# A 48-row first transform on quarters of the array, and expert weights loaded in pieces into buffers that the last batch frees

## The chip, the cores and the metric

The kernel runs on one core of a Trainium2 chip. The metric is device time in microseconds (us) of one execution. The core has TensorE (PE), VectorE (DVE), ScalarE (ACT), GpSimd (POOL) and SyncE (SP, here a queue that issues DMAs); 16 DMA engines carry data for all queues.

## What is computed

Three layers follow one another (shortened; the inputs are float32):

```python
X = np.fft.rfft(x, axis=1)                     # x: 8 x 3072 x 256
Yr = X.real @ w_r - X.imag @ w_i + b_r
Yi = X.real @ w_i + X.imag @ w_r + b_i
...                                            # both shrunk towards 0 by 0.01
y = np.fft.irfft(Y, n=3072, axis=1)            # 24576 tokens of 256
logits = y @ phi                               # 32 slots, 4 for each of 8 experts
slot_input = softmax(logits, 0).T @ y
slot_out[e] = np.maximum(slot_input[e] @ w1[e], 0) @ w2[e]   # 256 -> 1024 -> 256
z = softmax(logits, 1) @ slot_out
out = (silu(z @ w_gate) * (z @ w_val)) @ w_out # 256 -> 1536 -> 256
```

## The kernel before

**First half, up to about 584 us of the profile.** Eight batches of 3072 x 256 pass through a pipeline, one after another and overlapping. For each batch the 3072 points of a column are seen as 96 x 32. *Stage a* (`stage_a`, L586) is a float32 matmul with a fixed table `fwd`: 96 rows deep, 128 columns wide, 512 moving columns; it gives the 96-point transform of sixteen of the 256 columns, in one bank of the ring "ac" (two banks, shared with stage c). A DVE transpose (`turn`, L591) moves each bank into the buffer `chan`. A batch has 16 such pairs, p = 0 to 15. *Stage c* (L612) takes `chan` as weights and multiplies with the table `cm`, which finishes the transform; ACT and DVE split the result into a high and a low part (tiles `xg`, `sf`, `sg`). *Stage b* (L700, "pb") multiplies by the mixing weights in groups of three matmuls of 128 x 512 in a faster float format. Then follow the shrinking (ACT, and a join on POOL or DVE, L771), the product with `phi` (L797, four strips of 32 columns of the array side by side), DMAs that lay `yt` out as `yi` (L826), and per batch the logits, softmax and sums for the slots (L865 to L1122, L1103 in strips again). Float32 matmuls leave two records each in the trace, those of stage b one.

x is loaded by SP (L571), four tiles of 96 rows x 64 columns per batch, ring "xq" of two. The tables `cm` and `fwd` and the buffer `chan` lie in `apool`; x tiles in `xpool`.

**Expert weights.** w1 and w2 are 8 MB each. `load_w1` (L427) fetches a whole expert of w1 (1 MB) on POOL's queue: three into the room of `xpool`, freed after the last stage a, five into that of `apool`, freed after the last batch's stage c. `load_w2` (L432) fetches an expert of w2, also on POOL, into tiles that the last batch has left. POOL issues some of the last batch's yi copies too, in the same queue. Every queue tracks its DMAs with eight semaphores in turn, so that a DMA waits for the eighth before it.

**After the slots** (`after_slots`, to about 612 us) the experts run: L1435 with w1, a transpose (L1448), L1460 with w2. **Second half** (from 612 us): 576 steps of the gated layer, bound by PE, with their own loads. It keeps its text in the change.

**What sets the order.** The work of the first half is a list of tasks with the data they need; the table `ORDER` gives the sequence in which they are recorded, for all engines together, and each engine runs its own in that sequence. A negative entry picks the second engine of a task that has two. Waits follow from the data. `HOLD` tasks are dummy matmuls (L1387) that fill gaps near the end of the first half.

Of the kernel before, what the change touches and what calls it, by code (L numbers as in the profile page):

```python
# [23 lines left out]
R2 = 32  # L24
NCH = 24
# [7 lines left out]
def dft_tables():  # L33
# [7 lines left out]
    n1 = np.arange(R1)  # L41
    n2 = np.arange(R2)
    k2 = np.arange(R2)
    sign = np.where(k2 >= R2 // 2, -1.0, 1.0)
    alt1 = np.where(n1 % 2 == 0, 1.0, -1.0)
    alt2 = np.where(n2 % 2 == 0, 1.0, -1.0)
    k1 = np.array([[j, 23 + j] for j in range(NCH)])
    k1[0] = (0, 47)

    fwd = np.zeros((R1, 4, 32))  # L50
    mix = np.zeros((4, R2, NCH, 2, 2, R2))
    for j in range(NCH):
        for h in range(2):
            if j == 0 and h == 0:
                fwd[:, 0, 0] = 1.0
                fwd[:, 1, 0] = alt1
                for i in range(R2):
                    if i == 0:
                        mix[0, :, j, 0, h, 0] = 1.0
                        continue  # L60
                    src = 0 if i < 16 else 1
                    k = 96 * i if i < 16 else 48 + 96 * (i - 16)
                    a = 2 * np.pi * ((n2 * k) % n) / n
                    mix[src, :, j, 0, h, i] = np.cos(a)
                    mix[src, :, j, 1, h, i] = -np.sin(a)
                continue
            a = 2 * np.pi * ((n1 * k1[j, h]) % R1) / R1
            fwd[:, 2 * h, j] = np.cos(a)
            fwd[:, 2 * h + 1, j] = -np.sin(a)
            a = 2 * np.pi * ((n2[:, None] * (k1[j, h] + 96 * k2)[None, :]) % n) / n  # L70
            mix[2 * h, :, j, 0, h, :] = np.cos(a)
            mix[2 * h + 1, :, j, 0, h, :] = np.sin(a)
            mix[2 * h, :, j, 1, h, :] = -np.sin(a) * sign
            mix[2 * h + 1, :, j, 1, h, :] = np.cos(a) * sign
# [85 lines left out]
for _n, _w in (  # L160
# [11 lines left out]
FWD = 136  # L172
# [190 lines left out]
def kernel(  # L363
# [83 lines left out]
    def phase1():  # L447
# [1248 lines left out]
```

## Time and profile before

| what | us |
|---|---|
| runs | 1691.08, 1693.27, 1694.23; median 1693.27 |
| profiled execution | 1693.74 |
| its span in the trace | 1691.6 |
| PE busy in the span | 1662.7 (98%) |
| DVE, ACT, POOL busy | 1296.0, 980.7, 312.5 |
| start of the first matmul | 8.13 |
| start of the gated layer's first matmul | 612.05 |

The profile shows one execution. The rows below come from several of its views: the page (totals), windows (busy time of each engine in a stretch), the timeline (instructions in order, equal neighbours merged with a count), groups by line, and DMA issues. A matmul's own busy time overlaps the next one's, so the time that one costs is read from the starts of those around it. A name in brackets behind a row is what the instruction waited for.

### The profile page before, as it was taken

The page shows a single profiled execution, that of the slowest core. Times are in us where ns is not written, and L with a number is a line of the kernel's source. Part 1 is how long each engine was busy: PE and PEld are TensorE (multiplying, and loading weights), DVE is VectorE, ACT ScalarE, POOL GpSimd, SP SyncE. Part 2 cuts the span into 40 slices and gives each one's busy share as a digit, 9 for nine tenths or more (in the row PEclk, how much of TensorE's full clock was granted, in tenths as well). Part 3 has the DMA queues.
Part 4 walks back from the last instruction along what each step waited for, and adds up shares of the span by engine and source line. Part 5 has one row for each costly group of instructions (what it writes and reads, how often), then busy time and mean ns, then how long its engine had stood idle before and what let it go on. Part 6 is the DMA issues. An engine that isn't in the chain of part 4 may idle for free.

```text
span 1691.6 us, 23302 instructions
## 1 busy us (share of the span) xinstructions
PE 1662.7 (98%) x8178; PEld 1284.8 (76%) x8178; DVE 1296.0 (77%) x2203; ACT 980.7 (58%) x1830; POOL 312.5 (18%) x360
## 2 busy tenths in 40 slices
PE   7999999999999889999999999999999999999998
PEld 4677776776777558888888888888888888888886
DVE  5788888888778458778777777777777777877776
ACT  2655664655657246666656655665666656655664
POOL 1234433334444521100200200200010110110000
PEclk9999999999999999999999999999999999999999
DMA  9465666766556981311311311311230131131111
GB/s 193 88 139 120 123 123 144 138 142 122 126 132 216 310 200 26 81 26 26 81 19 20 82 25 26 70 37 25 41 66 15 24 81 26 25 72 26 25 26 25
DMA packets 260036, 139.94 MB, mean 83 GB/s; under 512 B 210224, under 2 KB 243728, under 8 KB 259920
## 3 DMA queue, kind: packets, MB, share of 16 engines
q1 hardware_dynamic: 246592, 105.03, 31.0%
q0 software_dynamic: 12272, 33.17, 7.2%
q8 instruction: 65, 1.06, 0.3%
q10 hardware_dynamic: 1056, 0.26, 0.1%
q14 instruction: 51, 0.42, 0.1%
HBM read 72.74 MB, written 40.50 MB: 67 GB/s over the span
## 4 chain that ended last, share of the span: by engine, by line
PE 94%; DMA 3%; DVE 1%; POOL 1%; ACT 0%; issue 0%; SPq 0%; DVEq 0%; ACTq 0%
PE o L1572 47%; PE pb L700 11%; PE pg L1547 8%; PE pv L1548 8%; PE ac L586 7%; PE ac L612 5%; PE ch L797 1%; PE ch L865 1%; PE ch L1055 1%; DMA w1s<-in_moe_w_dram 1%; PE ch L1103 1%; DMA w2s<-in_moe_w_dram 1%; PE ch L925 1%; PE ch L1011 1%; PE po L1460 1%; DMA xq<-in_x_dram 0%
## 5 line engine op out<-in xcount | busy, mean ns | idle before, releaser
L1572 PE MATMUL o<-hh,wo 128*128 128x512 f32 x2304 | 722.5, 395 | 0.0
L1550 ACT ACTIVATE sg<-pg 128x512 f32<-128x512 f32 x576 | 344.6, 598 | 413.8 <-PE pg L1547 413.8
L1552 DVE TENSOR_TENSOR h<-sg,pv 128x512 f32<-128x512 f32 x576 | 393.2, 683 | 248.6 <-ACT sg L1550 245.3
L1572 PEld LDWEIGHTS o<-hh,wo 128*128 128x128 f32 x2304 | 434.2, 188 | 100.8
L1572 PE MATMUL o<-hl,wo 128*128 128x512 f32 x1152 | 453.8, 394 | 0.0
L1560 DVE TENSOR_TENSOR hl<-h,hh 128x512 fp32r<-128x512 f32 x576 | 396.7, 689 | 0.1
L1559 ACT ACTIVATE hh<-h 128x512 fp32r<-128x512 f32 x576 | 359.4, 624 | 0.3 <-DVE h L1552 0.2
L1572 PEld LDWEIGHTS o<-hl,wo 128*128 128x128 f32 x1152 | 216.1, 188 | 51.9
L1547 PE MATMUL pg<-cst,gstk 96*128 96x512 f32 x576 | 227.7, 395 | 0.0
L1548 PE MATMUL pv<-cst,gstk 96*128 96x512 f32 x576 | 226.1, 393 | 0.6 <-DVE gstk L1533 0.6
L700 PE MATMUL pb<-xg,whl 128*128 128x512 f32 x576 | 179.3, 441 | 0.0
L700 PEld LDWEIGHTS pb<-xg,whl 128*128 128x128 f32 x576 | 105.3, 189 | 46.5 <-issue 25.1
L1548 PEld LDWEIGHTS pv<-cst,gstk 96*128 96x128 f32 x576 | 109.7, 190 | 25.9 <-DVE gstk L1533 0.9
L1547 PEld LDWEIGHTS pg<-cst,gstk 96*128 96x128 f32 x576 | 108.1, 188 | 25.7 <-DVE gstk L1533 0.8
L771 POOL TENSOR_TENSOR yt<-r,yt 128x512 f32<-128x512 f32 x74 | 96.6, 1305 | 153.5 <-ACT yt L762 103.2
L591 DVE STREAM_TRANSPOSE chan<-ac 128x512 f32<-128x512 f32 x128 | 89.8, 708 | 34.1 <-PE ac L586 29.8
L1608 POOL TENSOR_TENSOR e<-e,rs 96x256 f32<-96x256 f32 x28 | 22.6, 834 | 498.8 <-DVE rs L1605 498.8
L586 PE MATMUL ac<-xq,fwd 96*128 96x512 f32 x224 | 110.3, 598 | 1.2 <-DVE chan L591 0.7
L612 PEld LDWEIGHTS ac<-cm,chan 128*128 128x128 f32 x768 | 101.0, 196 | 12.1 <-issue 4.5
L612 PE MATMUL ac<-cm,chan 128*128 128x128 f32 x768 | 105.3, 283 | 0.0
L700 PE MATMUL pb<-sg,whl 128*128 128x512 f32 x288 | 86.7, 425 | 0.0
L634 ACT ACTIVATE sf<-ac 128x256 f32<-128x256 f32 x96 | 36.5, 381 | 78.5 <-PE ac L612 74.4
(151 smaller groups left out, 1481.1 us busy)
## 6 DMA issues: line engine op xcount, KB each, us to landing
out_dram<-ob SPq DMA_DIRECT2D x190, 128.0 KB, 2.8
yi<-yt SPq DMA_DIRECT2D x368, 64.0 KB, 2.1
xq<-in_x_dram SPq DMA_DIRECT2D x28, 768.0 KB, 8.1
cst<-c_scr POOLq DMA_DIRECT2D x72, 128.0 KB, 3.1
w1s<-in_moe_w_dram POOLq DMA_DIRECT2D x8, 1024.0 KB, 9.0
w2s<-in_moe_w_dram POOLq DMA_DIRECT2D x8, 1024.0 KB, 10.9
x<-in_x_dram SPq DMA_DIRECT2D x4, 768.0 KB, 10.1
cv<-in_moe_w_gate_dram SPq DMA_DIRECT2D x6, 512.0 KB, 6.0
```

What stands on the lines that cost most here:

```text
L586: nc.tensor.matmul(out=pt, lhsT=fwd[:, 8 - 8 * dh:136 - 8 * dh], rhs=T[kq][:, :, d1:d1 + 16], start=True, stop=True)
L591: nc.vector.transpose(out=chan[:, 12 * dh:12 * dh + 16, d0:d0 + 16, :].rearrange("p j d i -> p d j i"), in_=T[ka].rearrange("p n d -> p d n"),
L612: nc.tensor.matmul(out=pt[:, :, q:q + 2, i // 2, :], lhsT=chan[:, 16 * dh + j // 2, :, j % 2], rhs=cm[:, j, :].rearrange("p (c h k) -> p c ...
L700: nc.tensor.matmul(out=pt, lhsT=w[:, dh, m, es], rhs=xx, start=m != 1 and dh == 0 and n == 0, stop=dh == 1 and n == 2, skip_group_check=True,)
L771: e.tensor_sub(out=part(), in0=quarters(T[kr]), in1=part())
L1547: nc.tensor.matmul(out=pg, lhsT=gstk[:, 0, f * 128:(f + 1) * 128], rhs=rhs, start=True, stop=True)
L1548: nc.tensor.matmul(out=pv, lhsT=gstk[:, 1, f * 128:(f + 1) * 128], rhs=rhs, start=True, stop=True)
L1550: nc.scalar.activation(out=sg, in_=pg, func=AF.Silu)
L1552: nc.vector.tensor_mul(out=h, in0=sg, in1=pv)
L1559: nc.scalar.activation(out=hh, in_=h, func=AF.Copy)
L1560: nc.vector.tensor_sub(out=hl, in0=h, in1=hh.bitcast(F32))
L1572: nc.tensor.matmul(out=po_t[0][k], lhsT=w[:, f % 4, k * 128:(k + 1) * 128], rhs=a, start=(f == 0 and m == 0), stop=(f == NF - 1 and m == 2 ...
```

## The change

The 3072 points are now seen as 48 x 64. A first transform has 48 rows and 64 columns, so that it fits a quarter of the array; a batch's x comes in tiles of two row blocks (rows 0 to 47 and 64 to 111 of the tile), with two halves of 384 KB loaded apart, ring "xq" of three. For batches 1 to 7 one task issues four quarter matmuls, which fill two banks of "ac"; two turns follow. For batch 0 a task issues two quarter matmuls, one for each row block, into the two halves of one bank; half of batch 0's loads go out on ACT's queue. The tables `fwd` and `mix` are built to match; stage c and all that follows keep their shapes.

w1 is loaded in 16 halves of 512 KB: six into the room of the x tiles, seven into parts of `chan` and three into thirds of `cm`, each as soon as the last batch's reads of that part are recorded. Halves of w1 and experts of w2 may be issued by POOL or SP, as `ORDER` says. `apool` stays open until the experts have read w1. `ORDER` is new as a whole; it also holds 40 dummy matmuls instead of 36.

```diff
-FWD = 136
+FWD = 72
...
 ORDER = [
-    2, 1, 0, 3, 4, 5, 40, 30, 50, 312, 48, 49, 6, 8, 7, 9, 10, 12, 11, 13,
...
-    def load_w1(pool, e):
-        w1_t[e] = pool.tile([128, 2, FF], F32, tag="w1", name="w1s", bufs=3 if e < 3 else 5)
-        nc.gpsimd.dma_start(out=w1_t[e], in_=w1[e].rearrange("(k p) f -> p k f", p=128))
+    def load_w1(eng, t, e, k):
+        w1_t[e, k] = t
+        (nc.sync if eng == "SP" else nc.gpsimd).dma_start(out=t, in_=w1[e, 128 * k:128 * k + 128])
...
-            ("xq", 2), ("tt", 2), ("ac", 2), ("xg", 2), ("sf", 2), ("sg", 1), ("pb", 3), ("r", 1), ("yt", 2), ("yi", 4),
+            ("xq", 3), ("tt", 2), ("ac", 2), ("xg", 2), ("sf", 2), ("sg", 1), ("pb", 3), ("r", 1), ("yt", 2), ("yi", 4),
...
+        def half_x(k, r):
+            _, b, dh, c = k
+            d0 = 128 * dh + 64 * r
+            nc.sync.dma_start(
+                out=T[k][64 * r:64 * r + R0],
+                in_=x[b, :, d0:d0 + 64].rearrange("(p h n) d -> h p n d", h=2, n=R2)[c],
+            )
...
-        def stage_a(b, p, rank):
+        def stage_a0(dq, dd, rank):
...
             def mm():
                 pt = bank(ka, [128, R2, 16], "ac")
-                nc.tensor.matmul(
-                    out=pt, lhsT=fwd[:, 8 - 8 * dh:136 - 8 * dh], rhs=T[kq][:, :, d1:d1 + 16], start=True, stop=True
-                )
+                for r in range(2):
+                    rows = slice(64 * r, 64 * r + R0)
+                    nc.tensor.matmul(
+                        out=pt[64 * r:64 * r + 64], lhsT=fwd[rows, 8 - 8 * dh:72 - 8 * dh],
+                        rhs=T["x0", dq][rows, :, 16 * dd:16 * dd + 16], start=True, stop=True, skip_group_check=True,
+                    )
...
+        def stage_a(b, dh, dd, rank):
...
+            def mm():
+                pt = [bank(k, [128, R2, 16], "ac") for k in ka]
+                for r, c in ((0, 0), (1, 1), (0, 1), (1, 0)):
+                    rows = slice(64 * r, 64 * r + R0)
+                    nc.tensor.matmul(
+                        out=pt[r][64 * c:64 * c + 64], lhsT=fwd[rows, 8 - 8 * dh:72 - 8 * dh],
+                        rhs=T[kq[c]][rows, :, d1:d1 + 16], start=True, stop=True, skip_group_check=True,
+                    )
...
-        add("SP", free_a, r=["w1a"], w=["w1b"], after=both("xg", last, 2, 0) + both("xg", last, 2, 1) + ["xz"])
-        for e in range(E):
-            add(
-                "POOL", fetch_w1(e), r=["w1a" if e < 3 else "w1b"], w=[("w1", e)], after=[("yi", last, 0, 0) if e > 2 else ("cv", len(jobs) - 1)],
-            )
+        w1_at = [(e, k, None, ["w1a"]) for e in range(3) for k in range(2)]
+        for g in range(3):
+            seen = [("ac", "c", last, g, hb, dh) for hb in range(2) for dh in range(2)]
+            seen += [("ch", "z", last, dh) for dh in range(2 * (g == 0))]
+            for dh in range(2):
+                j = 4 * g + 16 * dh
+                w1_at.append((3 + g, dh, chan[:, j:j + 4].rearrange("p j d i -> p (j d i)"), seen))
+            w1_at.append((6 + g // 2, g % 2, cm[:, 8 * g:8 * g + 8].rearrange("p j k -> p (j k)"), seen))
+        w1_at.append((7, 1, chan[:, 12:16].rearrange("p j d i -> p (j d i)"), [("tt", last, p // 8, p) for p in range(16)]))
+        both_q = ("POOL", "SP")
+        for e, k, at, seen in w1_at:
+            add(both_q, fetch_w1(e, k, at), w=[("w1", e, k)], after=seen)
...
-            add("POOL", fetch_w2(e), w=[f"w2{e}"], new=(new, f"w2{e}") if new else None, after=behind)
+            add(both_q, fetch_w2(e), w=[f"w2{e}"], new=(new, f"w2{e}") if new else None, after=behind)
...
-        close_pool("w1b", "w1a")
+        close_pool("w1a", "apool")
```

How the instructions stand now is shown at three places. A row is a line of the kernel, an operation, the tile written and those read, the shape, and a count.

PE, second half of batch 1's first transforms ("ac<-xq"), among stage b of batch 0 ("pb"); before:

```order
L586 MATMUL ac<-xq,fwd 128x512 x2
L700 MATMUL pb<-xg,whl 128x512 x3
L586 MATMUL ac<-xq,fwd 128x512 x2
L700 MATMUL pb<-xg,whl 128x512 x3
L586 MATMUL ac<-xq,fwd 128x512 x2
L655 MATMUL ch<-csm,chan 128x2
L586 MATMUL ac<-xq,fwd 128x512 x2
L797 MATMUL ch<-yt,phis 32x256 x8
L655 MATMUL ch<-csm,chan 128x2
```

and now (L643, L765, L862 are what L586, L700, L797 were):

```order
L643 MATMUL ac<-xq,fwd 64x512 x4
L765 MATMUL pb<-xg,whl 128x512 x6
L643 MATMUL ac<-xq,fwd 64x512 x4
L765 MATMUL pb<-xg,whl 128x512 x3
L862 MATMUL ch<-yt,phis 32x256 x4
L643 MATMUL ac<-xq,fwd 64x512 x4
L765 MATMUL pb<-xg,whl 128x512 x3
L765 MATMUL pb<-sg,whl 128x512 x3
L643 MATMUL ac<-xq,fwd 64x512 x4
L862 MATMUL ch<-yt,phis 32x256 x4
```

Before, eight full-height matmuls stand in four pairs; now four groups of four quarters stand apart, with three or six pb or a block of strips between them, and the strips are cut in two.

POOL's queue, the first loads of w1 ("w1s") and w2 ("w2s") among the last batches' joins; before:

```order
L427 DMA w1s<-in_moe_w_dram 128x2x1024
L771 TENSOR_TENSOR yt<-r,yt 128x4x128
L427 DMA w1s<-in_moe_w_dram 128x2x1024
L771 TENSOR_TENSOR yt<-r,yt 128x4x128
L650 TENSOR_TENSOR sg<-sf,sg 128x4x64 x2
L771 TENSOR_TENSOR yt<-r,yt 128x4x128
L432 DMA w2s<-in_moe_w_dram 128x2x1024
L771 TENSOR_TENSOR yt<-r,yt 128x4x128
L851 TENSOR_TENSOR p_5006<-vt,csm 128x384
L427 DMA w1s<-in_moe_w_dram 128x2x1024
L851 TENSOR_TENSOR p_5006<-vt,csm 128x384
L427 DMA w1s<-in_moe_w_dram 128x2x1024 x2
```

and now ("chan" and "cm" are written by halves of w1):

```order
L442 DMA w1s<-in_moe_w_dram 128x1024 x2
L715 TENSOR_TENSOR sg<-sf,sg 128x4x64 x2
L442 DMA chan<-in_moe_w_dram 128x1024
L442 DMA cm<-in_moe_w_dram 128x1024
L442 DMA w1s<-in_moe_w_dram 128x1024
L836 TENSOR_TENSOR yt<-r,yt 128x4x128
L715 TENSOR_TENSOR sg<-sf,sg 128x4x64 x2
L916 TENSOR_TENSOR p_5169<-vt,csm 128x384 x2
L836 TENSOR_TENSOR yt<-r,yt 128x4x128
L442 DMA chan<-in_moe_w_dram 128x1024
L836 TENSOR_TENSOR yt<-r,yt 128x4x128
L447 DMA w2s<-in_moe_w_dram 128x2x1024
```

Two whole experts of w1 stood ahead of the other six; now POOL holds halves, in part into `chan` and `cm`, ahead of the rotation products (p).

SP's queue at the same place, yi copies and stores ("e_scr", "w_scr"); before:

```order
L826 DMA yi<-yt 32x2x256 x16
L1176 DMA e_scr<-ls 96x1024
L1246 DMA w_scr_61<-cv 256x1x128 x2
L1246 DMA w_scr_62<-cv 256x1x128 x2
L826 DMA yi<-yt 32x2x256 x24
L1176 DMA e_scr<-ls 96x1024
L826 DMA yi<-yt 32x2x256 x8
L443 DMA wg<-w_scr_59 128x2x512
```

and now:

```order
L891 DMA yi<-yt 32x2x256 x16
L442 DMA w1s<-in_moe_w_dram 128x1024
L1241 DMA e_scr<-ls 96x1024
L442 DMA chan<-in_moe_w_dram 128x1024
L1311 DMA w_scr_61<-cv 256x1x128 x2
L1311 DMA w_scr_62<-cv 256x1x128 x2
L891 DMA yi<-yt 32x2x256 x16
L1266 DMA cv<-in_moe_w_out_dram 128x2x512
L442 DMA w1s<-in_moe_w_dram 128x1024
L442 DMA cm<-in_moe_w_dram 128x1024
L891 DMA yi<-yt 32x2x256 x16
L442 DMA w1s<-in_moe_w_dram 128x1024
```

SP carried no expert weights; now halves of w1 stand between its blocks of 16 yi copies, and three experts of w2 behind the last of them.

## Rows read from the trace of the kernel before

**Rows 1.** The page: busy time by engine (part 1), the last chain by engine (part 4).

```profile
PE 1662.7 (98%) x8178; PEld 1284.8 (76%) x8178; DVE 1296.0 (77%) x2203; ACT 980.7 (58%) x1830; POOL 312.5 (18%) x360
...
PE 94%; DMA 3%; DVE 1%; POOL 1%; ACT 0%; issue 0%; SPq 0%; DVEq 0%; ACTq 0%
```

**Rows 2.** Windows from 40 to 540 us, the row of sums: busy us of each engine.

```profile
sum 500.00, PE 497.45 PEld 360.57 DVE 419.51 ACT 296.00 POOL 186.32; mean PE 71.06 PEld 51.51 DVE 59.93 ACT 42.29 POOL 26.62
```

**Rows 3.** Timeline, POOL and PE: start, us, engine, line, operation, tiles, count, [wait].

```profile
517.84 0.90 POOL L427 DMA_DIRECT2D w1s<-in_moe_w_dram  x1
...
540.50 0.76 POOL L427 DMA_DIRECT2D w1s<-in_moe_w_dram  x1
...
569.80 1.60 POOL L826 DMA_DIRECT2D yi<-yt  x3 [5.50 <-DMA w1s<-in_moe_w_dram]
...
572.95 1.64 PE L1055 MATMUL ch<-vpad,csm 128*128 128x192 f32 x8 [2.80 <-DVE vpad L1044]
...
574.84 2.93 PE L1055 MATMUL ch<-vpad,csm 128*128 128x192 f32 x8
...
580.62 2.37 PE L1103 MATMUL ch<-yi,p 128*32 128x256 f32 x40 [1.13 <-DMA w2s<-in_moe_w_dram]
...
595.05 3.17 PE L1460 MATMUL po<-w2s,h1t 128*32 128x256 f32 x25 [3.21 <-DMA w2s<-in_moe_w_dram]
...
603.14 3.66 PE L1460 MATMUL po<-w2s,h1t 128*32 128x256 f32 x64
```

**Rows 4.** Windows: stretch, length, busy of PE, PEld, DVE, ACT, POOL; clock, DMA share, GB/s.

```profile
500.00:540.00 40.00, 40.00 (x241) 31.91 (x240) 33.71 (x71) 29.38 (x61) 15.26 (x16) 1.00 0.58 176
570.00:580.00 10.00, 6.69 (x48) 5.40 (x46) 3.32 (x7) 0.98 (x2) 3.86 (x7) 0.83 0.98 262
540.00:600.00 60.00, 51.61 (x431) 34.18 (x429) 29.89 (x70) 14.96 (x25) 27.34 (x36) 0.94 0.93 313
```

**Rows 5.** Timeline, PE, first transforms of batch 1 among pb; counts are records.

```profile
74.18 2.96 PE L700 MATMUL pb<-xg,whl 128*128 128x512 f32 x12
76.98 1.88 PE L586 MATMUL ac<-xq,fwd 96*128 96x512 f32 x4
...
79.40 1.88 PE L586 MATMUL ac<-xq,fwd 96*128 96x512 f32 x4
```

**Rows 6.** Timeline, PE: matmuls into 64 columns each (two halves).

```profile
608.47 3.65 PE L1522 MATMUL pq<-wg,tail 128*64 128x512 f32 x16 [0.38 <-DVE tail L1505]
```

**Rows 7.** Timeline, PE, around a block of 32-column strips.

```profile
540.81 0.86 PE L700 MATMUL pb<-xg,whl 128*128 128x512 f32 x3
541.60 1.07 PE L797 MATMUL ch<-yt,phis 128*32 128x256 f32 x16
542.60 4.47 PE L700 MATMUL pb<-xg,whl 128*128 128x512 f32 x18
546.91 0.33 PE L1055 MATMUL ch<-vpad,csm 128*128 128x192 f32 x1
```

**Rows 8.** Timeline, DVE: two turns; groups by line (count, busy us, mean ns, idle before).

```profile
78.04 1.57 DVE L591 STREAM_TRANSPOSE chan<-ac 128x512 f32<-128x512 f32 x2 [0.71 <-PE ac L586]
...
L771 POOL TENSOR_TENSOR yt<-r,yt 128x512 f32<-128x512 f32 x74 | 96.6, 1305 | 153.5 <-ACT yt L762 103.2 <-ACT r L762 29.3 <-DMA xq<-in_x_dram 10.7
...
L771 DVE TENSOR_TENSOR yt<-r,yt 128x512 f32<-128x512 f32 x22 | 15.0, 683 | 5.0 <-ACT r L762 2.6 <-ACT yt L762 2.2
...
L650 POOL TENSOR_TENSOR sg<-sf,sg 128x256 fp32r<-128x256 f32 x74 | 55.6, 755 | 99.2 <-ACT sg L646 92.3 <-DMA yi<-yt 4.7 <-issue 1.1
...
L650 DVE TENSOR_TENSOR sg<-sf,sg 128x256 fp32r<-128x256 f32 x22 | 9.4, 429 | 1.8 <-ACT sg L646 1.2 <-issue 0.5
```

**Rows 9.** DMA issues: tile, queue, count, KB each, us to landing.

```profile
xq<-in_x_dram SPq DMA_DIRECT2D x28, 768.0 KB, 8.1
```

**Rows 10.** Timeline, PE: the first transforms of batch 0, and what follows.

```profile
8.13 17.36 PE L586 MATMUL ac<-x,fwd 96*128 96x512 f32 x30 [8.13 <-DMA fwd<-in_csmall_dram]
25.44 2.15 PE L612 MATMUL ac<-cm,chan 128*128 128x128 f32 x16
```

More of the change, by code (lines that the diff above doesn't have):

```diff
@@ L24 @@
 R2 = 32
+R0 = 48
 NCH = 24
@@ L45, in dft_tables, with put_mix @@
     alt1 = np.where(n1 % 2 == 0, 1.0, -1.0)
+    alt0 = np.where(m1 % 2 == 0, 1.0, -1.0)
     alt2 = np.where(n2 % 2 == 0, 1.0, -1.0)
[L47 to L51, printed above, removed]
-    for j in range(NCH):
+    k1 = np.array([[j, 48 + j] for j in range(NCH)])
+    k1[0] = (0, 24)
+    fwd = np.zeros((R0, 2, 32))
+    mix = np.zeros((2, 2, R2, NCH, 2, 2, R2))
+    def put_mix(part, j, c, h, i, v):
+        mix[:, part, :, j, c, h, i] = v.reshape((2, R2) + v.shape[1:])
@@ L53, in dft_tables @@
+    every = slice(None)
+    for j in range(NCH):
+        if j == 0:
+            fwd[:, 0, 0] = 1.0
+            fwd[:, 1, 0] = alt0
+        else:
+            a = 2 * np.pi * ((m1 * j) % R0) / R0
+            fwd[:, 0, j] = np.cos(a)
+            fwd[:, 1, j] = -np.sin(a)
         for h in range(2):
             if j == 0 and h == 0:
[L55 to L61, printed above, removed]
+                put_mix(0, j, 0, h, 0, np.ones(2 * R2))
+                for i in range(1, R2):
@@ L69, in dft_tables @@
[L69 to L74, printed above, removed]
+            a = 2 * np.pi * ((m2[:, None] * (k1[j, h] + 96 * k2)[None, :]) % n) / n
+            if j == 0:
+                put_mix(1, j, 0, h, every, np.cos(a))
+                put_mix(1, j, 1, h, every, -np.sin(a) * sign)
+                continue
@@ L76, in dft_tables @@
+            put_mix(0, j, 0, h, every, np.cos(a))
+            put_mix(1, j, 0, h, every, np.sin(a))
+            put_mix(0, j, 1, h, every, -np.sin(a) * sign)
+            put_mix(1, j, 1, h, every, np.cos(a) * sign)
     kn = 2 * np.pi * (np.outer(k2, n2) % R2) / R2
@@ L131, in dft_tables @@
     last[0:32, 0] = alt2
+    last[64:96, 0] = alt2
     fold = np.tile(np.eye(32), (4, 4))
@@ L551, in phase1, with load_first @@
         add("DVE", setup_small, w=["small", "vpad", "M"])
-        def load_first(dq):
+        def load_first(dq, r):
             def go():
-                T["x0", dq] = t = early.tile([R1, R2, 64], F32, name=f"x0{dq}")
-                nc.sync.dma_start(
-                    out=t, in_=x[0, :, dq * 64:(dq + 1) * 64].rearrange("(p n) d -> p n d", n=R2)
+                if ("x0", dq) not in T:
+                    T["x0", dq] = early.tile([64 + R0, R2, 64], F32, name=f"x0{dq}")
+                (nc.sync, nc.scalar)[r].dma_start(
+                    out=T["x0", dq][64 * r:64 * r + R0],
+                    in_=x[0, :, 64 * dq:64 * dq + 64].rearrange("(p h n) d -> h p n d", h=2, n=R2)[r],
                 )
@@ L594, in turn, with go @@
                 )
-            add("PE", mm, r=["f", kq, kt], w=[ka], new=[("ac", ka)] + ([("tt", kt)] if p % 8 == 0 else []))
-            add("DVE", turn, r=[ka], w=[(*kt, p)])
+            kt = ("tt", 0, dh)
+            add(
+                "PE", mm, r=["f", kt] + [("x0", dq, r) for r in range(2)], w=[ka], new=[("ac", ka)] + ([("tt", kt)] if d0 == 0 else []),
+            )
+            add("DVE", turn, r=[ka], w=[(*kt, 4 * dq + dd)])
+        def stage_a(b, dh, dd, rank):
+            kq = [("xq", b, dh, c) for c in range(2)]
+            kt = ("tt", b, dh)
+            ps = [8 * dh + 4 * r + dd for r in range(2)]
+            ka = [("ac", "a", b, p) for p in ps]
+            d1 = dd * 16
+            def mm():
[5 more added lines that the diff above has]
+                        rhs=T[kq[c]][rows, :, d1:d1 + 16], start=True, stop=True, skip_group_check=True,
+                    )
+            def turn(r):
+                def go():
+                    d0 = 64 * r + d1
+                    nc.vector.transpose(
+                        out=chan[:, 12 * dh:12 * dh + 16, d0:d0 + 16, :].rearrange("p j d i -> p d j i"),
+                        in_=T[ka[r]].rearrange("p n d -> p d n"),
+                    )
+                return go
+            add(
+                "PE", mm, r=["f", kt] + [(*k, r) for k in kq for r in range(2)], w=ka, new=[("ac", k) for k in ka] + ([("tt", kt)] if dd == 0 else []),
+            )
+            for r in range(2):
+                add("DVE", turn(r), r=[ka[r]], w=[(*kt, ps[r])])
         def stage_c(b, g, hb, dh, rank):
@@ L1298, in phase1 @@
             for dq in range(4 * (b == 0)):
-                add("SP", load_first(dq), w=[("x0", dq)])
-            for dq in range(4):
-                if b == 0 and dq == 3:
+                for r, q in enumerate(("SP", "ACT")):
+                    add(q, load_first(dq, r), w=[("x0", dq, r)])
+                if dq == 3:
                     constants(0)
-                if b:
-                    add("SP", load_x(b, dq), w=[("xq", b, dq)], new=("xq", ("xq", b, dq)))
-                for p in range(4 * dq, 4 * dq + 4):
-                    stage_a(b, p, a0 + p * da)
+                for dd in range(4):
+                    stage_a0(dq, dd, a0 + (4 * dq + dd) * da)
+            for dh in range(2 * (b > 0)):
+                for c in range(2):
+                    k = ("xq", b, dh, c)
+                    t = a0 - 1.0 + (8 * dh + 4 * c) * da
+                    add("SP", load_x(k), w=[(*k, 0)], new=("xq", k))
+                    add("SP", load_x2(k), w=[(*k, 1)])
+                for dd in range(4):
+                    stage_a(b, dh, dd, a0 + (8 * dh + 2 * dd) * da)
             if b == 0:
```

55 lines of the change are left out of this document (27 added, 28 removed), and 240 rows, old and new, of the table ORDER.

## The prediction, made before the changed kernel was run

> **What bounds the kernel now.** I read the page first: TensorE is busy for 98% of the span, and the chain that ended last lies on it for 94% [rows 1]. So the question is which of its time goes away, and what comes late in its place. The windows come next: from 40 to 540 us, where seven of the eight batches pass through the first transform, PE is busy for 497 of 500 us and DVE for 420 (84%), ACT for 296, POOL for 186 [rows 2]. PE is the bound there, with DVE 80 us behind. After 540 us it is another matter: rows with a wait in brackets show PE standing [rows 3], while the DMA engines, busy for 0.58 in the 40 us ahead, are at 0.98 [rows 4]. The second half of the kernel, from 612 us, is not touched by the diff, and I take its time as it is.
>
> **The first transform, on the quarters.** What one costs is read from the timeline, since a matmul's own busy time overlaps its neighbour's. Twelve pb matmuls take 76.98 - 74.18 = 2.80 us, 0.233 each. From 76.98 to 79.40 stand two first transforms (four records, two for each float32 matmul) and three pb: 2.42 - 0.70 = 1.72, so 0.86 each [rows 5]. Batches 1 to 7 have 112 of them: 96.3 us. After the change 56 groups of four quarter matmuls do the same work, each with the same 512 moving columns. If the four run side by side a group takes 0.86, in all 48.2 us, and **48 us go**.
>
> Do they run side by side? Two halves of the columns do: eight 128x512 matmuls into 64 columns each took 3.65 us, where one after the other they would take 8 x 0.86 = 6.9 [rows 6]; and four strips of 32 columns do: eight 128x256 matmuls, 0.43 each alone, took 1.00 us instead of 3.4 [rows 7]. All of these read the full height of the array. That two halves of the rows also work at once, no row shows. The bounds are 0.86 us for a group (all four at once) and 1.72 (the row halves in turn, column halves together), and I take 0.86, since the nearest rows show the array split with no loss at all.
>
> **What a split costs.** Each time the array goes from one shape to another, PE loses a little. Three pb ahead of an L797 block take 541.60 - 540.81 = 0.79 instead of 0.70: 0.09 lost. The block's four rounds take 1.00 instead of 4 x 0.214 = 0.86: 0.14 lost. The 18 pb behind it take 4.31 instead of 18 x 0.233 = 4.19: 0.12 lost [rows 7]. That is 0.35 for two changes of shape, 0.17 each. I counted them in the two orders, up to the end of the slots: 111 before, 236 after, since nearly every group stands alone between full-height work, and strips of 32 columns that stood in one block are now often cut in two. **125 more at 0.17 are 21 us back.** The bounds are 0.09 (the loss ahead of the block alone, 11 us) and twice the row's (42 us), since no row has a shape that is split by rows at this size; I take 21. The Trainium skill, TensorEngine Tiling (Array Packing), section Key Properties, says that a change of the tiling mode, not of the tile alone, drains the engine, which speaks against scattering 56 groups; the 0.09 agrees with it. Were changes of shape free, the sum below would end 21 us lower, near 1646.
>
> **Who waits for whom around a group.** A group fills both "ac" banks at once. Before the next user of both can start, two DVE turns must pass, 1.57 us together [rows 8], and a few tenths for the two hand-overs. By the new order's rows, 17 of the 37 pairs of neighbouring groups have less other work between them than these 1.9 us (most have six pb, 1.4 us, and two changes of shape): some 0.2 us is missing in each, **3 us**. Beside this, DVE has the same turns, but 12 low parts of the sums and 9 joins go from DVE to POOL: 12 x 0.43 + 9 x 0.68 = 11.3 us, less two other operations of about 0.7 that come the other way, so 10 us. On POOL they cost 12 x 0.76 + 9 x 1.31 = 21 us [rows 8], which its 37% leaves room for. DVE then has 410 us of work in a stretch of some 475: 86% instead of 84%. I put **3 us** more on PE for that, with 0 and 12 as the bounds (12 is where DVE would have to be busy for 84% as now).
>
> The x tiles: a ring of three in place of two; each tile comes in two halves. The last tile of a batch needs the slot of the first, so its load starts after the batch's fourth group, and the order leaves PE 9 to 13 us of other work before the fifth. A load lands in 8.1 us [rows 9]. It fits, narrowly; 0 to 1 us for each of seven batches lies within the bound above. The 28 further issues on SP cost about 0.6 each on a queue that mostly waits; the yi copies behind them are wanted many us later. In batch 0 a pair of quarters does what one matmul did, so nothing is gained; there the 15 first ones take (25.44 - 8.13) / 15 = 1.15 each [rows 10], more than 0.86, because DVE's turns set the pace, and this stays. The four loads on ACT's queue stand ahead of anything ACT computes.
>
> Body: -48 + 21 + 3 + 3 = **-21 us**.
>
> **The weights.** Before, w1 goes out from POOL in whole experts, two from 517.84 on and the other six from 540.50 on [rows 3]. Now 16 halves go out from POOL and SP as soon as each third of the last batch's buffer and table has been read. In 500 to 540 the DMA engines stand idle for 0.42 of 40 us [rows 4], which is 17 us of carrying, so some 5 MB (at the 313 GB/s that a share of 0.93 carried from 540 to 600) can move ahead. What waits for DMA at the end now: PE stands 3.21 us for w2, and its clock falls, so that 25 matmuls behind take 3.17 us where 64 take 3.66 at the end: 1.7 lost. Earlier POOL is stuck behind its own DMA lanes until 569.80, its product for the rotation comes late, PE stands 2.80 us, and eight matmuls take 2.9 us instead of 1.6, with the granted clock at 0.83 in this stretch, so part of it at 1.2 GHz. Then 1.13 us for the last yi copies [rows 3, 4]. That is 3.2 + 1.7 + 2.8 + 1.3 + 1.1 = 10 us. The first two should go, as the weights land earlier; of the others perhaps a quarter, because POOL's last product still stands behind 16 yi copies and three loads, each waiting for the eighth DMA before it. **-6 us**, between 0 and -10. The 40 filler matmuls instead of 36 fill waits only.
>
> **Sum.** The profiled execution took 1693.74 us, 0.5 above the median of the three runs. 1693.7 - 21 - 6 = 1666.7: **1667 us**.
>
> **Rivals.** (1) *DVE becomes the bound.* For: 86% on one engine with every group waiting for two of its turns. Against: the order leaves only 3 us missing. If DVE cannot exceed 84%, the stretch is 410 / 0.84 = 488 us, a gain of 12 and with the weights 18: 1676; with late x tiles too, 1680.
> (2) *Batch 0 in series.* Its two row halves write the same bank (in later batches, different banks). A pair then takes 1.72 instead of 1.15 for 15 pairs: +8.6, 1675. The Trainium skill, TensorEngine Tiling (Array Packing), Gotcha 1: PSUM Pressure, says that different row tiles cannot use the same PSUM bank at the same time. No row shows it either way; against it stands that the two write different partitions.
> (3) *Changes of shape cost double* for a split by rows: +21, 1688.
> (4) *Slower: the row halves do not run at once.* A group costs 1.72, nothing is saved, the 21 us of changes stay, batch 0 loses 8.6, the turns are covered, the weights give 6: 1693.7 + 21 + 8.6 - 6 = 1717. It decides from the point where a group takes 1.34 us: then 56 x 0.38 = 21 saved is what changes of shape and turns (27) less the weights (6) cost. For it: no row shows two row halves at once. Against: column halves share the same rows and lose nothing, and here the row halves read different partitions. The Trainium skill, TensorE: Matmul & The Clock Gate, Part 3, reports four row strips running at 3.07 times one; no run here shows it.
>
> **How the numbers follow.** Forecast 55%, with 1652 to 1676 (the weights at -10 and changes at 0.09 at one end, DVE and x tiles late at the other). Rival 1: 17%. Rival 2: 12%. Rival 3: 7%. Rival 4: 9%. The range 1652 to 1684 leaves out rival 4, most of rival 3 and the tails, about 2 in 10. Within 0.2% (3.4 us, about what a measurement of this kernel can tell from no change) lies only the upper end of rival 3: 3%. Slower: rival 4, 9%. Faster: 88%.
>
> **What would show it.** In the new profile the four quarter matmuls of a group should start within some hundredths of a microsecond of each other, twice, 0.43 apart; pb behind a group should show one long interval. If the second pair of quarters starts 0.43 or 0.86 later, rival 4 holds. In batch 0 the turns should still come 0.8 to 1.15 apart. DVE should be near 86% in the body; waits of PE for chan or xq show rival 1. At the end, PE's wait for w2 should be gone. The forecast is wrong if DVE rises above 90% with PE waiting, or if 0.17 is not the price.

## The result: slower by 0.8%, and the profile after

The changed kernel takes 1706.8 us (median of four runs, 1704.01 to 1709.76); the kernel before, timed beside it, 1693.75 us. The ratio is 1.0081, with a 95% interval of 1.0068 to 1.0094. The forecast was 1667 us, with 1652 to 1684 as its range: wrong in sign. The profiled execution took 1706.88 us, 13.1 more than that of before.

The page after, parts 1 and 4, beside [rows 1] (here the chain of part 4 is followed back only into the second half, 64% of the span):

```profile
PE 1658.0 (97%) x8442; PEld 1256.4 (74%) x8442; DVE 1288.9 (76%) x2184; ACT 980.5 (58%) x1830; POOL 324.6 (19%) x375
...
PE 64%; DVE 0%; ACT 0%; issue 0%; DVEq 0%
```

Windows after (columns as in [rows 4]), beside [rows 2, 4]:

```profile
0.00:25.00 25.00, 13.45 (x39) 3.45 (x40) 7.11 (x14) 1.28 (x1) 0.70 (x6) 0.95 1.27 117
...
40.00:540.00 500.00, 483.50 (x3128) 328.08 (x3127) 407.86 (x728) 292.53 (x589) 198.95 (x188) 0.99 0.79 129
...
580.00:600.00 20.00, 13.44 (x102) 11.30 (x106) 6.50 (x12) 4.18 (x8) 6.52 (x9) 0.83 0.88 266
```

and the body before, whole row:

```profile
40.00:540.00 500.00, 497.45 (x2902) 360.57 (x2902) 419.51 (x751) 296.00 (x590) 186.32 (x174) 1.00 0.61 130
```

In the body PE stands for 16.5 of 500 us where it stood for 2.5, DVE is busy for 408 us instead of 420, and the DMA engines are busy for 0.79 of the time, to carry what 0.61 carried before (129 GB/s here, 130 there). Three marks tell where the time went: the starts of the first pb, of the last pb, and of the first matmul of the second half.

| us | before | after | difference | forecast |
|---|---|---|---|---|
| start, up to the first pb | 29.3 | 40.3 | +11.0 | 0 |
| body, first to last pb | 517.4 | 523.5 | +6.1 | -21 |
| tail, to the second half | 65.4 | 61.6 | -3.8 | -6 |
| second half | 1079.6 | 1079.8 | +0.2 | 0 |

The start, PE's timeline after, beside [rows 10]:

```profile
10.00 10.18 PE L615 MATMUL ac<-x,fwd 48*64 48x512 f32 x32 [10.00 <-DMA fwd<-in_csmall_dram]
20.85 1.04 PE L615 MATMUL ac<-x,fwd 48*64 48x512 f32 x2 [0.67 <-DMA x<-in_x_dram]
22.76 12.21 PE L615 MATMUL ac<-x,fwd 48*64 48x512 f32 x26 [0.88 <-DMA x<-in_x_dram]
34.90 3.78 PE L677 MATMUL ac<-cm,chan 128*128 128x128 f32 x16
```

and the clock in it, from windows after:

```profile
16.00:20.50 4.50, 4.17 (x18) 0.78 (x16) 3.29 (x6) 0.00 (x0) 0.00 (x0) 1.00 1.41 121
...
24.00:35.00 11.00, 11.00 (x25) 2.87 (x22) 4.31 (x6) 0.00 (x0) 0.00 (x0) 0.50 1.19 259
```

PE begins 1.9 us later, waits for x twice, and then runs at a granted clock of 0.50 (1.2 GHz) from 22.4 to 39.5 us: sixteen matmuls of the second transform take 3.78 us, where [rows 10] has 2.15. At half the clock these 17.1 us do what 8.5 would at the full one, but that is not what the fall costs: a run below has the same loads at full clock, and there PE stands for x instead.

A group in the body (the four quarter matmuls of one task), PE's timeline after:

```profile
73.59 1.66 PE L765 MATMUL pb<-xg,whl 128*128 128x512 f32 x6
75.18 1.09 PE L643 MATMUL ac<-xq,fwd 48*64 48x512 f32 x8
76.20 0.64 PE L862 MATMUL ch<-yt,phis 128*32 128x256 f32 x8
...
145.27 1.53 PE L643 MATMUL ac<-xq,fwd 48*64 48x512 f32 x8
146.74 0.97 PE L765 MATMUL pb<-xg,whl 128*128 128x512 f32 x3
```

The first group's four quarters start within 0.02 us of each other, and their second passes 0.48 later: the row halves do run at once. The group takes 76.20 - 75.18 = 1.02 us. The group at 145.27 takes 1.47: its second bank comes 0.45 us late. In all, 15 of 56 groups take over 1.06 us, 9.3 us more than 1.02 each.

The x loads, first 5 to 18 us, of before and then of after (queue: packets, MB, share of 16 engines):

```profile
q1 hardware_dynamic: 8719, 2.24, 139.1%
```

```profile
q1 hardware_dynamic: 3308, 0.84, 76.4%
q10 hardware_dynamic: 2937, 0.74, 64.4%
```

The DMA engines are full in both (a share over 100% means packets that overlap), but carry 2.24 MB in one and 1.58 in the other. A packet's time is the share times 16 engines times 13 us over the packets: 33 ns before, 47 after. Both are packets of 256 bytes. In the body the packets of 256 bytes, which are those of x alone, take 28 and 41 ns.

### The profile page after: what moved, and what is told of

Read it like the earlier page. It is cut to its first block, busy times and chain, and to the rows that moved or that the text cites. A ratio compares the mean times of both kernels' runs of the same rounds, so it can differ in the third digit from the quotient of the medians.

```text
span 1705.1 us, 23860 instructions
## 1 busy us (share of the span) xinstructions
PE 1658.0 (97%) x8442; PEld 1256.4 (74%) x8442; DVE 1288.9 (76%) x2184; ACT 980.5 (58%) x1830; POOL 324.6 (19%) x375
## 4 chain that ended last, share of the span: by engine, by line
PE 64%; DVE 0%; ACT 0%; issue 0%; DVEq 0%
PE o L1646 47%; PE pg L1621 8%; PE pv L1622 8%; PE po L1534 0%; PE ph L1509 0%; PE pq L1596 0%; PE ch L1120 0%; PE ch L1168 0%; PE pt L1522 0%; DVE ob L1653 0%; DVE gstk L1607 0%; ACT gstk L1602 0%; PE pb L1461 0%; PE psot L1578 0%; PE pst L1494 0%
## 5 line engine op out<-in xcount | busy, mean ns | idle before, releaser
L765 PE MATMUL pb<-xg,whl 128*128 128x512 f32 x576 | 167.9, 422 | 5.0 <-ACT yt L817 3.7
L765 PEld LDWEIGHTS pb<-xg,whl 128*128 128x128 f32 x576 | 103.3, 191 | 57.1 <-issue 22.7
L836 POOL TENSOR_TENSOR yt<-r,yt 128x512 f32<-128x512 f32 x83 | 108.6, 1309 | 169.4 <-ACT yt L827 108.2
L1621 PEld LDWEIGHTS pg<-cst,gstk 96*128 96x128 f32 x576 | 108.1, 188 | 25.6 <-DVE gstk L1607 0.8
L651 DVE STREAM_TRANSPOSE chan<-ac 128x512 f32<-128x512 f32 x112 | 74.0, 694 | 22.7 <-PE ac L643 22.2
L715 POOL TENSOR_TENSOR sg<-sf,sg 128x256 fp32r<-128x256 f32 x86 | 63.8, 751 | 124.8 <-ACT sg L711 102.4
L693 ACT ACTIVATE xg<-ac 128x512 fp32r<-128x512 f32 x96 | 56.2, 594 | 51.3 <-DVE sf L702 36.2
L765 PE MATMUL pb<-sg,whl 128*128 128x512 f32 x288 | 82.8, 418 | 0.0
```

Of the source, the lines that this page charges most:

```text
L651: nc.vector.transpose(out=chan[:, 12 * dh:12 * dh + 16, d0:d0 + 16, :].rearrange("p j d i -> p d j i"), in_=T[ka[r]].rearrange("p n d -> p ...
L715: e.tensor_sub(out=sview(1), in0=T[ks], in1=sview(0).bitcast(F32))
L765: nc.tensor.matmul(out=pt, lhsT=w[:, dh, m, es], rhs=xx, start=m != 1 and dh == 0 and n == 0, stop=dh == 1 and n == 2, skip_group_check=True,)
L836: e.tensor_sub(out=part(), in0=quarters(T[kr]), in1=part())
L1621: nc.tensor.matmul(out=pg, lhsT=gstk[:, 0, f * 128:(f + 1) * 128], rhs=rhs, start=True, stop=True)
```

## Experiments

Six theories, numbered in the expectations, were put to runs: that the loads are slow because of their 48 partitions (1), of their source rows (2), or of where the tile begins in each partition (4); that the body lost its gain to VectorE (3) or to the order (5); and that the tail's new wait is SP's lateness (6). Tile addresses are those of the built kernels. Packet times are given as "start / body" (5 to 18 and 60 to 500 us).

**Batch 0 whole.** Loads and transform of batch 0 as before: one full-height matmul for each pair.

```diff
-                for r in range(2):
-                    nc.tensor.matmul(out=pt[64 * r:64 * r + 64], lhsT=fwd[rows, ...], rhs=T["x0", dq][rows, ...], ...)
+                nc.tensor.matmul(out=pt, lhsT=fwd0[:, 8 - 8 * dh:136 - 8 * dh], rhs=T["x0", dq][:, :, 16 * dd:16 * dd + 16], ...)
```

> The changed kernel, with batch 0 alone undone: its four x tiles are loaded whole into 96 partitions by SP as in the kernel before, and one full-height matmul (a table of 96 rows with the two halves' rows in turn and zeros between) takes the place of each pair of quarters; batches 1 to 7, order and weights stay. Theory 1: the start's whole 11 us come from batch 0's loads and from the clock that falls while TensorE waits for them: first pb at 29 to 31 us, granted clock 1.00 between 20 and 40 us, time 1694 to 1698 us. Rival (the pace is set later by VectorE and its banks, which have slack to catch up after a late start): time 1701 to 1707 us although the first pb is early.

Measured 1684.1 us, ratio 0.9938 (0.9924 to 0.9953): twice the gain expected, and faster than both kernels. The start came back (first pb 29.3), but the body fell too, from 523.5 to 513.1 us, and x packets in it from 41 to 25 ns, though its loads were not touched. What had moved was their place: the second table pushed the x tiles of batches 1 to 7 from 32 bytes past a multiple of 64 to a multiple of 512. Neither theory had that.

**Partitions and source rows.** Before, with split loads; and after, with other source rows.

```diff
-                    out=t, in_=x[...]
+                    out=t[u:u + 48], in_=x[...][u:u + 48]      # for u in (0, 48)
```

> The kernel before, with every load of an x tile (96 partitions, 768 KB) cut into two loads of 48 partitions; nothing else differs. Theory 1 (a load into 48 partitions moves less per microsecond than one into 96): the 256-byte x packets of the first 18 us, 33 ns each in the kernel before and 47 ns in the changed one, take 43 to 50 ns; the first pb matmul moves from 29.3 us to 36 to 41 us, as in the changed kernel (40.3), and the time is 1700 to 1706 us. Theory 2 (the changed kernel's loads are slow because their source rows come in every other block of 32): the packets stay at 33 ns, the first pb at 29 to 31 us, the time 1693 to 1696 us.

> The changed kernel, with each half tile of x read from 48 blocks of 32 rows that follow each other, instead of every other block; the packets, their number and where they land are the same, but the rows are the wrong ones for the transform. Theory 1 (48 partitions): x packets stay at 46 to 48 ns in the first 18 us and near 41 ns between 200 and 300 us, time 1704 to 1710 us. Theory 2 (source stride): 33 and 28 ns, first pb at 29 to 31 us, time below 1697 us.

The split cost the kernel before 17 us: 1712.0 us, packets 43 / 38 ns. The source rows cost nothing: 1706.3 us, 47 / 41 ns, as in the changed kernel. Theory 2 fell. Theory 1 held for the packets and in direction, but 1712.0 us is 6 more than it gave, the first pb (35.5 us) came a little before its 36 to 41, and it could not explain the fast halves of the run above.

The run with other source rows also parts the loads from the clock. Its start, and the clock in it:

```profile
25.24 3.83 PE L615 MATMUL ac<-x,fwd 48*64 48x512 f32 x16 [2.90 <-DMA x<-in_x_dram]
30.66 2.97 PE L615 MATMUL ac<-x,fwd 48*64 48x512 f32 x12 [1.59 <-DMA x<-in_x_dram]
...
37.88 1.08 PE L765 MATMUL pb<-xg,whl 128*128 128x512 f32 x3
```

```profile
18.00:30.00 12.00, 8.17 (x36) 1.76 (x32) 6.89 (x10) 0.00 (x0) 0.00 (x0) 1.00 1.35 136
```

Here the clock is at 1.00, PE stands 4.5 us for x, and the first pb comes at 37.88 us all the same, 8.6 us later than before. So the late loads alone keep the start back by most of the 11 us. What the fall of the clock adds in the changed kernel is an estimate from these rows: 40.25 - 37.88 = 2.4 us, and up to 5.2 if the later first matmul of this run (12.84 us, for 10.00) counts in full.

**The tile's address.** Padding only.

```diff
-        fwd = apool.tile([64 + R0, FWD], F32, name="fwd")
+        fwd = apool.tile([64 + R0, 80], F32, name="fwd")[:, 0:FWD]
         early = open_pool("early")
+        early.tile([128, 56], F32, name="spare")
```

> The changed kernel with nothing but padding: the x tiles of all batches now begin, within each partition, at a multiple of 512 bytes, where in the changed kernel (and in the kernel before) they begin 32 bytes past a multiple of 64. Loads, partitions, order and arithmetic stay. Theory 4 (a load of 256-byte pieces into 48 partitions is slow only when the pieces straddle a boundary in the tile's memory): x packets take 25 to 33 ns in every stretch instead of 47 and 41 ns, first pb at 29 to 31 us instead of 40.3, body as in the run with batch 0 whole (513 us), time 1680 to 1687 us. Rival (half-height loads are slow by themselves, and the run with batch 0 whole was faster in its body only because it started early): packets 38 to 47 ns, first pb 36 to 41 us, time 1698 to 1708 us.

Measured 1681.15 us, ratio 0.9926 (0.9911 to 0.9941), 25.6 us less than the changed kernel. Its first 18 us, and its start:

```profile
q10 hardware_dynamic: 4943, 1.25, 72.3%
q1 hardware_dynamic: 4295, 1.09, 60.2%
```

```profile
7.50 17.48 PE L616 MATMUL ac<-x,fwd 48*64 48x512 f32 x60 [7.50 <-DMA fwd<-in_csmall_dram]
24.91 2.15 PE L678 MATMUL ac<-cm,chan 128*128 128x128 f32 x16
```

About the same engine time now carries 2.34 MB, at 30 ns a packet; PE does not wait for x and keeps its clock over these rows. The padding moves `fwd` and `cm`, which lie in the same pool, along with the x tiles; that it is the loads which count rests on their own packets. In the body:

```profile
40.00:540.00 500.00, 488.54 (x3188) 333.63 (x3188) 419.08 (x743) 300.81 (x600) 207.61 (x199) 1.00 0.62 138
```

The DMA share is back at 0.62. Start 29.2, body 511.3, tail 60.5 us.

> The kernel before with each x load cut in two loads of 48 partitions (which cost 17 us), now with the x tiles at multiples of 512 bytes. Theory 4 (straddling): x packets back to 25 to 33 ns, time 1692 to 1698 us. Rival (48 partitions): packets 38 to 43 ns, time 1704 to 1712 us.

> The kernel before with whole loads, only its x tiles at multiples of 512 bytes. Theory 4: its 96-partition packets, 33 and 28 ns, get a little shorter (25 to 30 ns); TensorE does not wait for x there except at the start, so the time is 1690 to 1695 us, no change. Rival (the address costs the kernel before as much as the changed one): under 1685 us.

The split loads in the kernel before, aligned: 1694.97 us, 23 / 23 ns, so the 17 us are gone but for some 3. Whole loads, aligned: 19 / 18 ns, shorter than the 25 to 30 expected, 1691.8 us, ratio 0.9984 (0.9974 to 0.9994). The misplaced tiles cost the kernel before some 2.6 us; its PE waits 0.4 us for x in the body. So neither the 48 partitions nor the address cost much by itself; both together did. Both with aligned tiles, the change is worth 1691.82 - 1681.15 = 10.7 us.

> The changed kernel with padding that puts the x tiles 64 bytes past a multiple of 128 (batch 0) and 192 bytes past a multiple of 256 (the others): multiples of 64, not of 128, where the run with aligned tiles had multiples of 512. If a multiple of 64 bytes is all that the loads need, x packets take 25 to 33 ns and the time is 1679 to 1685 us as with 512. If the pieces have to begin at a multiple of their own 256 bytes, packets take 38 to 47 ns and the time is 1700 to 1708 us.

> The changed kernel, padded so that the x tiles begin 128 bytes past a multiple of 256. At 32 past 64 the packets took 47 ns at the start and 41 ns later, at 64 past 128 they took 42 and 35, at multiples of 512 they took 30 and 25. If a multiple of 128 is all that a 256-byte piece needs: 30 and 25 ns, 1679 to 1685 us. If it has to begin at a multiple of 256: 33 to 42 ns, 1686 to 1696 us.

| x tiles begin | 96 partitions, ns | 48 partitions, ns | changed kernel, us |
|---|---|---|---|
| 32 past a multiple of 64 | 33 / 28 | 47 / 41 | 1706.8 |
| 64 past a multiple of 128 | | 42 / 36 | 1693.1 |
| 128 past a multiple of 256 | | 42 / 35 | 1689.9 |
| a multiple of 512 | 19 / 18 | 30 / 25 | 1681.2 |

Multiples of 64 and of 128 are alike and lie between, so neither branch of the first of these expectations came true, and the second branch of the other did. Of the places tried only the multiple of 512 is quick; 256 past 512 was not tried, so whether 256 is enough stays open. The runs at 64 and 128, like those with split loads and other source rows, are single and have no interval.

**VectorE in the body.** Turns cut to half their columns; misaligned, then aligned, then with the turns of y cut as well.

```diff
-                        out=chan[:, ..., d0:d0 + 16, :], in_=T[ka[r]]
+                        out=chan[:, ..., d0:d0 + 8, :], in_=T[ka[r]][:, :, 0:8]
```

> The changed kernel, with each turn of batches 1 to 7 on VectorE cut to half its columns (0.70 us to about 0.38 us, 112 of them, so VectorE has some 36 us less to do and each bank comes free 0.3 us earlier); the other half of the transform's output is left out. Theory 3 (the body lost its gain to TensorE waiting for banks and tiles that VectorE hands over): groups that take over 1.06 us instead of 1.02 fall from 15 of 56 to under 5, TensorE's standing between 40 and 565 us from 17.9 us to under 8, time 1685 to 1693 us. Rival (late x tiles and a slower DMA hold the body back): time 1702 to 1708 us, the same waits.

> The changed kernel with aligned x tiles, and with each turn of batches 1 to 7 on VectorE cut to half its columns (half of the transform's output is left out): VectorE has some 36 us less to do and the banks come free 0.3 us earlier. It asks what is left of TensorE's waits once the loads are quick. Theory 3 (waits for banks that VectorE empties): 6 to 12 us less than with aligned tiles alone, 1670 to 1679 us, late groups under 5 of 56. Rival (the waits left are set by the order of work and by chains over several engines, not by the turns): within 3 us of aligned tiles alone, 1678 to 1687 us.

> The changed kernel with aligned x tiles, the turns of batches 1 to 7 cut to half their columns, and the turns of y in place, 1.22 us each, cut to a small part too; half of the transform's output and nearly all of the turned y are left out. VectorE, busy for 428 us between first and last pb with aligned tiles and for 403 with the transform's turns halved, falls to 350 to 365 us. If VectorE's pace makes what the body still loses, TensorE's standing in the body falls from 12 us to under 5 and the body from 511 us to 496 to 503. If the waits are chains over several engines at places that the order sets, the body stays at 505 to 509 us, as with the halved turns alone (508).

Measured 1704.5 us (ratio 1.0064, 1.0042 to 1.0086), 1679.7 us (0.9916, 0.9896 to 0.9937) and 1673.8 us (a single run). Theory 3 fails for the misaligned kernel, where 16 groups are late instead of 15. With aligned tiles the body goes from 511.3 to 508.1 and 504.7 us, while VectorE's busy time in it falls from 428 to 403 and 357; late groups are 12, 13 and 12 of 56, and PE's standing falls from 12.3 to 10.5 and 7.7 us. Seventy us off VectorE buy 6.6 us, a little past the bound that the last expectation set for chains; so VectorE has a part, and the smaller one.

**The order.** The table rearranged by a search, aligned tiles.

> The changed kernel with aligned x tiles and another order of the same tasks: a search over the table, with each kind of task at the duration that the run with aligned tiles shows, moved tasks so that TensorE waits less (in the search's own account 26 us less, of which some 22 are waits and 4 are 24 fewer changes of shape, 196 for 220); x loads and weight loads keep their order, and 14 low parts of the sums go back from GpSimd to VectorE. Theory 5 (what the body still loses with aligned tiles, some 17 us, is TensorE standing at places that the order sets, not VectorE's pace): the time between first and last pb falls from 511 us to 492 to 500 us and the whole to 1662 to 1672 us. Rival (VectorE's pace, which a new order cannot mend and 14 more tasks on it make worse): 1678 to 1685 us.

Measured 1765.5 us (ratio 1.0418). The search had moved work without counting what holds SP. Waits of PE, then of SP's queue, in that run:

```profile
PE pb L766 <- ACT yt L818: 30.4, 7, 11.0
PE ac L644 <- DMA xq<-in_x_dram: 15.9, 7, 4.8
```

```profile
SPq L892 <- DVE yt L879: 132.0, 15, 16.6
```

and one group's yi copies on SP, with aligned tiles in the old order:

```profile
53.90 10.34 SPq L892 DMA_DIRECT2D yi<-yt  x16
64.70 1.07 SPq L590 DMA_DIRECT2D xq<-in_x_dram  x2
```

Sixteen issues hold SP for 10.3 us. Where they wait for a late turn of y, x loads wait behind them, and PE behind those: 63 us of standing in the body, where the old order has 12, and some 30 lost to the clock (PE's busy time in 75 us at 1.2 GHz, halved).

> The changed kernel with aligned x tiles and a second search for an order, whose account now holds what the first new order (1765 us) showed to be missing: the sixteen yi copies of a group hold SP for some 10.4 us, not 2, and everything behind them on SP waits, x loads above all. In this account the order with aligned tiles ends at 571 us and the first new order near 600, as measured to within some 15 us of each, and this one at 547. Theory 5 (the 17 us that the body still loses are waits set by the order): body 492 to 502 us, time 1658 to 1672 us. Rival (the pace of VectorE and SP, whatever the order): 1677 us or more.

Measured 1688.9 us (0.9972, 0.9961 to 0.9982): 7.7 us slower than the old order with aligned tiles, and in the rival's range. Its body is 513.6 us, with 17.2 us of standing, at other places. The search's account put it 24 us ahead of the old order (547 for 571), so it is too coarse for a gain of this size. Nor does this run change the order alone: VectorE is busy for 450 us of the body where it was busy for 428. Theory 5 is not shown. How much of the remaining loss an order could mend is left open.

**The tail.** The store of the logits on ScalarE's queue.

```diff
-                nc.sync.dma_start(out=e_scr[b], in_=...)
+                (nc.scalar if b == B - 2 else nc.sync).dma_start(out=e_scr[b], in_=...)
```

> The changed kernel with aligned x tiles; the one store of the next-to-last batch's logits to scratch goes out on ScalarE's queue, right behind the work that makes them, instead of on SP behind eight yi copies. Theory 6 (the wait of TensorE for the logits' tile at the end, 4.8 us in the run with aligned tiles, and the clock of 1.2 GHz behind it, 3.4 us lost, are new costs of the weights' new order, since SP is late with that store): the wait falls under 2 us and the time by 3 to 7 us, to 1674 to 1678 us. Rival (the store lands late anyway, because the DMA engines are full of weights): 1679 to 1683 us.

> The two edits above together. If both theories hold they add: 1656 to 1668 us. If the store was late only because of the order, this is as fast as the new order alone, within 2 us.

Measured 1682.3 us (0.9926, 0.9908 to 0.9944), no gain, within the rival's range; with the first new order 1764.5 us, as without. PE's waits in the tail, aligned tiles and then this run:

```profile
PE ch L1041 <- ACT ls L1011: 4.8, 1, 4.8
```

```profile
PE ch L1041 <- ACT ls L1011: 1.0, 1, 1.0
...
PE ch L1121 <- DVE vpad L1110: 4.3, 1, 4.3
```

The wait fell as theory 6 said, and the next one, for a product that GpSimd makes behind its own DMAs, took its place.

## Why the prediction was wrong, step by step

**Quarters, 48 us: right.** A group is 1.02 us, and the six pb ahead of it take 75.18 - 73.59 = 1.59 instead of 1.40. That is 1.21 us with two changes of shape; the forecast had 0.86 + 0.34 = 1.20. Rival 4, whose 1717 us is nearest to the result, is refuted in its mechanism. So is rival 2. VectorE's turns of batch 0 after:

```profile
16.43 0.72 DVE L621 STREAM_TRANSPOSE chan<-ac 128x512 f32<-128x512 f32 x1 [0.29 <-PE ac L615]
17.34 0.72 DVE L621 STREAM_TRANSPOSE chan<-ac 128x512 f32<-128x512 f32 x1 [0.20 <-PE ac L615]
```

They come 0.91 us apart at full clock; two row halves of one bank in turn would need 1.72. The Trainium skill, TensorEngine Tiling (Array Packing), Gotcha 1: PSUM Pressure, says that different row tiles cannot use the same bank at once. Here two halves that write different partitions of one bank do, and the measurement decides.

One reading was wrong without harm: that VectorE's turns set batch 0's pace of 1.15 us. In the kernel before, each turn or pair of turns waits for PE:

```profile
11.93 0.72 DVE L591 STREAM_TRANSPOSE chan<-ac 128x512 f32<-128x512 f32 x1 [0.99 <-PE ac L586]
...
16.92 1.57 DVE L591 STREAM_TRANSPOSE chan<-ac 128x512 f32<-128x512 f32 x2 [0.36 <-PE ac L586]
```

The 1.15 are an average: the turns start 1.71 us apart up to 13.63 us, and some 0.97 after that.

**Changes of shape, 21 us: right.** Counting columns, the work between first and last pb is 45 us less (the 48, and 3 us of other work that moved in), and 125 changes at 0.17 give 21 back; the 0.17 is what the group above shows, 0.35 for two.

**"It fits, narrowly": the step that failed.** The forecast priced the x loads by their issue alone, with 0 for what they cost the DMA engines and 0 to 1 us a batch for tiles that come late, and took the landing of 8.1 us for 768 KB as if nothing in it changed with the halves. The halves of 384 KB take as long as the whole tiles did, and less with aligned tiles (after, then aligned):

```profile
xq<-in_x_dram SPq DMA_DIRECT2D x56, 384.0 KB, 8.3
```

```profile
xq<-in_x_dram SPq DMA_DIRECT2D x56, 384.0 KB, 6.3
```

Halves of 48 partitions in a misaligned tile make it so, and padding alone takes 25.6 us of the 39.8 us between forecast and result away: some 11 in the start, 12 in the body, the rest in the tail. In the body x loads and yi copies share SP's queue. Waits of SP's yi copies for x loads between 60 and 545 us, after and then aligned:

```profile
SPq L891 <- DMA xq<-in_x_dram: 18.8, 11, 2.7
```

```profile
SPq L892 <- DMA xq<-in_x_dram: 3.1, 4, 1.1
```

Copies that go out late free `yt` late, and ScalarE stands for them (none of this with aligned tiles):

```profile
ACT yt L817 <- DMA yi<-yt: 6.3, 3, 2.5
```

So PE's own waits for x in the body are short, 1.3 us, and the loads reach it by way of other engines. No part of the sum looked at batch 0's loads, though [rows 10] begins with a wait for DMA. Two sections of the Trainium skill bear on it. The Trainium skill, SBUF — State Buffer, section Door 1: The DMA port swizzle, says that bandwidth depends on how many of 16 ports the partitions reach; by its formula partitions 0 to 47 reach half of them. The trace agrees in kind: 18 ns into 96 partitions, 23 to 25 into 48. And the Trainium skill, DMA: Bandwidth & Descriptors, section How a descriptor splits into AXI transactions, lets a transaction start only at a multiple of 256 bytes, so that a piece of 256 bytes which begins elsewhere takes two; it speaks of reads, and here it is the address written that was moved. The table above agrees in part: 64 and 128 are alike and 512 is quick, but 32 past 64 is slower than both, which that section does not give.

**Waits, 3 + 3 us: too small.** After, the body's sum is -45 + 21 + 30 = +6. The 30 are what is left over, and 29 of them are found: PE standing (17.9 instead of 3.4 us, 14.5), the clock (four stretches of 3.4 us at 1.2 GHz, 6.8), and second banks that come late (some 7 of the 9.3; the others are in the standing and the clock already). With aligned tiles they are 18: 8.9, 1.7 and 5.8 found. That leaves 12 us of error that the address does not explain. Rival 1 named VectorE's 86%; it is busy for 82%, and taking 70 us off it gave 6.6. What makes the rest is not shown: the rows name chains over two or three engines, and in the second new order they stand at other places. Neither of the prediction's two signs of being wrong appeared, a VectorE above 90% or another price than 0.17.

**Tail, -6: -3.8.** The wait for w2 is gone, as forecast. New is one for the logits' tile, 5.48 us, and a stretch of 6.8 us at 1.2 GHz that begins within it:

```profile
585.24 0.53 PE L1040 MATMUL ch<-dg,ones 32*96 32x32 f32 x2 [5.48 <-ACT ls L1010]
```

ScalarE waits there for a store that SP issues at 575.24, behind eight yi copies, and that lands 9.2 us later among the weights.

```profile
575.24 0.34 SPq L1241 DMA_DIRECT2D e_scr<-ls  x1
...
584.59 1.08 ACT L1010 ACTIVATE ls<-ch 96x512 f32<-96x512 f32 x2 [12.54 <-DMA e_scr<-ls]
```

With aligned tiles the changed kernel takes 1681 us, inside the range, but not by the forecast's sum: the profiled executions differ by -45 + 21 + 18 = -6 us in the body, where -21 was forecast, by -5 in the tail and by 0 in the start. That the range holds it is partly luck, since its upper end was set by other rivals than the waits that fill it.

## What to carry to other kernels

Where a change resizes a tile, look at what it does to the addresses of all tiles behind it and to the partitions that each DMA writes: here the trace showed it as a DMA share that rose from 0.61 to 0.79 while the bytes stayed the same. A transfer that "fits narrowly" is worth a bound of its own, with what it costs when it does not fit, the clock included. And a part that is right to 1% (here 1.21 us for a group) says nothing of the sum.

## What the runs showed of the hardware

- Packets of 256 bytes into 48 partitions took 41 ns where the tile began 32 bytes past a multiple of 64, 36 or 35 at 64 past a multiple of 128 or 128 past one of 256, and 25 at a multiple of 512; into 96 partitions 28 (32 past) and 18 (512).
- Four quarters of the array ran at once: two passes of 512 columns started 0.48 us apart, and a group took 1.02 us with its change of shape. Two row halves that write different partitions of one PSUM bank ran at once too (0.91 us a pair).
- Two short waits of PE for x in batch 0 (0.67 and 0.88 us) were followed by 17 us at 1.2 GHz; in the run with other source rows waits of 2.90 and 1.59 us at the same place were followed by none, the granted clock being 1.00 from 18 to 40 us. In the changed kernel's body there were four stretches of 3.4 us at 1.2 GHz.
- Sixteen DMA issues of 64 KB each held SP for 10.3 us.
